# Taking all 512 columns in one matrix instruction in the projections and the first output product

## The chip, the cores and the metric

The program runs on one core of a Trainium2 chip. The time is device microseconds (us) of that core, the median of three runs. In the profile PE is the matrix engine (TensorE), PEld its weight loads, DVE is VectorE, ACT is ScalarE, POOL is GpSimd and SP issues the DMA transfers. PEclk is the clock that TensorE was granted, as a share of 2.4 GHz.

## The reference

Eight heads of attention in chunks of 64 positions give 4608 tokens of 512 features; two feed-forward layers follow. Cut to what matters:

```python
scores = q_c @ k_c.T / sqrt(64)              # per head and chunk of 64
attn = softmax(scores); x = attn @ v_c       # x: 4608 x 512
h = max(max(x @ w1, x @ w2), x @ w3)         # w1..w3: 512 x 768
y = h @ w_out                                # 768 x 512
g = max(y @ w_in, 0); g = g * g              # w_in: 512 x 2048
out = g @ w_out2                             # 2048 x 512
```

## The kernel before

The tokens are worked in nine blocks `b` of 512 (`TB`). Every product is made in three passes: each operand is split into a high part and a low part, both stored as fp32r, and high x high, high x low and low x high are added up in PSUM.

A *projection* is `proj` (L381): for one of six slices `f` of 128 features of h and one of the three matrices `w`, four blocks `k` of the inner dimension times three passes, into one PSUM tile `p` of 128 x 512. There are 9 x 6 x 3 = 162 of them, and two PSUM tiles `p`, used in turn. `p1_end` (L400) reads each tile out: `w` = 0 by a copy on ACT (L404), `w` = 1 by a maximum on DVE (L407), `w` = 2 by a maximum on DVE (L411), after which h is split into `hh` (ACT, L414) and `hl` (DVE, L416). The *first output product* is `g2` (L423): for each `(b, f)` four tiles `y` times three passes, added up over f in four PSUM tiles; after f = 5 they are copied out and sent to memory as `ys` (L433 to 438).

Both go through `mm_k` and `halves` (L365 to 379). `halves` takes each pass in pieces of `HC` = 256 columns, so a 512-column tile takes two instructions with the same stationary operand `lhs`, and each of them brings its own load of these weights. Two of the 162 projections, `(0, 0, 0)` and `(0, 0, 1)`, are called with `parts=2`: they are computed for each half of the block by itself, so there `dst` has 256 columns and `halves` makes one instruction per pass.

The later products, `z` (L461, y x w_in) and `g4` (L514, g x w_out2), write their own loops over 256 columns and do not go through `halves`. They use seven products for eight (a Strassen scheme), whose combined weights are prepared beforehand by `park` (L186; POOL adds at L161, ACT and DVE split at L210 and L212), stored, and fetched by `fetch` (L216) late in the projections.

The order: to about 165 us the order of all engines is written out by hand as a string of tokens. After that, `g2` and projections follow in loops over b and f, with one step of attention (scores S at L286, exponentials L293 to 299, sums L305 to 310, scaling on POOL at L313, transposition T at L319, output X at L347) beside each f, and the order within each engine is the framework's. The z products begin at about 675 us and the g4 products at about 1024 us. `heat` (L587) issues a few 128 x 512 bf16 products of zeros at the beginning.

Of the kernel before, what the change touches and what calls it, by code (L numbers as in the profile page):

```python
# [24 lines left out]
HC = 256  # L25
# [16 lines left out]
def kernel(ctx: ExitStack, tc, qkv, w123, w_out, w_in2, w_out2, out):  # L42


    nc = tc.nc
# [319 lines left out]
    def mm_k(dst, wpair, xpair, k, first, last):  # L365

        (wh, wl), (xh, xl) = wpair, xpair
        halves(dst, ((wh, xh), (wh, xl), (wl, xh)), first, last)

    def halves(dst, pairs, first, last):  # L370


        for j, (lhs, rhs) in enumerate(pairs):
            for i in range(dst.shape[-1] // HC):
                c = slice(i * HC, i * HC + HC)
                nc.tensor.matmul(  # L376
                    dst[:, c], lhsT=lhs, rhs=rhs[:, c], start=first and i == 0 and j == 0,
                    stop=last and j == len(pairs) - 1, skip_group_check=True,
                )

    def proj(wpair, xpair, name, parts=1):  # L381

# [215 lines left out]
    first = tc.manual_schedule()  # L598
# [138 lines left out]
    last = None  # L737
    more = iter(())
    for b in range(NB):
        for g in range(NG):  # L740
# [20 lines left out]
            last = (a, (b, g))  # L761
# [79 lines left out]
```

## Time and profile before

| what | value |
|---|---|
| runs | 1372.63 us median (1372.28 to 1373.52) |
| profiled execution: its own time | 1373.2 us |
| profiled execution: span | 1371.4 us, mean granted clock 0.997 |
| PE busy | 1356.9 us (99%), 13697 instructions |
| PEld busy | 1343.4 us (98%), 13699 instructions |
| DVE, ACT, POOL busy | 66%, 38%, 14% |
| DMA | 222.33 MB, mean 162 GB/s |

Busy time is the union of the records of an engine. Records of consecutive matrix instructions overlap, so the busy share of PE says that it had work, and the distance between two starts says how fast it went. In the views, `xN` at the end of a row is the number of instructions that it stands for.

### The profile page before, as it was taken

To read this page: it belongs to the slowest core of one execution; us is meant where nothing else is said; L and a number is where in the kernel's file an instruction comes from. 1 tells how busy PE (TensorE), PEld (TensorE's weight loads), DVE (VectorE), ACT (ScalarE), POOL (GpSimd) and SP (SyncE) were. 2 spreads that over 40 slices of the span, in tenths; PEclk is the share of its full clock that TensorE was granted. 3 is DMA by queue.
4 is the path that set the end of the run, shared out by engine and by line. 5 is a ranking of instruction groups with operands and counts; after the bars stand their busy time and mean duration, and the time that the engine had idled before them with its cause. 6 is when DMAs were issued, how large, how long until landed. Compare 5 with 4: busy or idle time off the path is not lost.

```text
span 1371.4 us, 32653 instructions
## 1 busy us (share of the span) xinstructions
PE 1356.9 (99%) x13697; PEld 1343.4 (98%) x13699; DVE 901.9 (66%) x1437; ACT 520.4 (38%) x904; POOL 194.5 (14%) x180
## 2 busy tenths in 40 slices
PE   7999999999999999999999999999999999999998
PEld 5999999999999999999999999999999999999998
DVE  7875565665665566622376666667667888878774
ACT  4643243343333333311233333333334444444442
POOL 3321133221432332300000000000000000000000
PEclk9999999999999999999999999999999999999999
DMA  9342353654644645617643334333598444444341
GB/s 280 123 137 81 124 182 125 227 159 154 213 142 166 219 140 180 220 55 239 198 148 124 129 141 147 139 139 141 189 345 315 149 146 132 131 139 149 130 139 46
DMA packets 101235, 222.33 MB, mean 162 GB/s; under 512 B 11232, under 2 KB 20448, under 8 KB 101088
## 3 DMA queue, kind: packets, MB, share of 16 engines
q1 hardware_dynamic: 101088, 220.25, 47.9%
q8 instruction: 107, 1.75, 0.5%
q14 instruction: 40, 0.33, 0.1%
HBM read 134.22 MB, written 85.98 MB: 161 GB/s over the span
## 4 chain that ended last, share of the span: by engine, by line
PE 86%; DVE 1%; issue 0%; POOLq 0%; POOL 0%; ACT 0%; DVEq 0%; ACTq 0%
PE z L471 25%; PE p L376 25%; PE o L522 25%; PE y L376 9%; PE X L347 1%; PE S L286 1%; PE T L319 1%; DVE pl L212 0%; DVE u L494 0%; POOL u L494 0%; POOLq L837 0%; DVE c L494 0%; DVE mx L293 0%; DVE sm L305 0%; DVE e L296 0%
## 5 line engine op out<-in xcount | busy, mean ns | idle before, releaser
L471 PE MATMUL z<-yxh,wih 128*128 128x256 f32 x560 | 155.4, 278 | 0.0
L471 PE MATMUL z<-yxh,wil 128*128 128x256 f32 x560 | 155.1, 277 | 0.0
L471 PE MATMUL z<-yxl,wih 128*128 128x256 f32 x560 | 155.1, 277 | 0.0
L522 PE MATMUL o<-wo2h,gl 128*128 128x256 f32 x504 | 139.2, 276 | 0.0
L522 PE MATMUL o<-wo2h,gh 128*128 128x256 f32 x504 | 139.2, 276 | 0.0
L522 PE MATMUL o<-wo2l,gh 128*128 128x256 f32 x504 | 139.2, 276 | 0.0
L522 PE MATMUL o<-wo2h,gxl 128*128 128x256 f32 x504 | 139.1, 276 | 0.0
L522 PE MATMUL o<-wo2l,gxh 128*128 128x256 f32 x504 | 139.1, 276 | 0.0
L522 PE MATMUL o<-wo2h,gxh 128*128 128x256 f32 x504 | 139.1, 276 | 0.0
L494 DVE TENSOR_TENSOR c<-z,s 128x512 f32<-128x512 f32 x108 | 74.4, 689 | 89.3 <-PE z L471 84.7
L414 ACT CAST hh<-h 128x512 fp32r<-128x512 f32 x54 | 33.4, 621 | 241.9 <-DVE h L411 223.8
L471 PE MATMUL z<-yh,wih 128*128 128x256 f32 x448 | 124.0, 277 | 0.0
L471 PE MATMUL z<-yh,wil 128*128 128x256 f32 x448 | 123.7, 276 | 0.0
L471 PE MATMUL z<-yl,wih 128*128 128x256 f32 x448 | 123.7, 276 | 0.0
L411 DVE TENSOR_TENSOR h<-p,m 128x512 f32<-128x512 f32 x54 | 37.1, 689 | 130.9 <-PE p L376 130.8
L494 POOL TENSOR_TENSOR u<-u,s 128x512 f32<-128x512 f32 x9 | 11.7, 1297 | 753.9 <-DVE u L494 753.9
L479 ACT COPY s<-z 128x512 f32<-128x512 f32 x108 | 63.5, 588 | 134.2 <-PE z L471 104.1
L471 PEld LDWEIGHTS z<-yxh,wih 128*128 128x128 f32 x560 | 105.3, 188 | 0.2 <-DVE c L494 0.2
L471 PEld LDWEIGHTS z<-yxl,wih 128*128 128x128 f32 x560 | 105.4, 188 | 0.0
L471 PEld LDWEIGHTS z<-yxh,wil 128*128 128x128 f32 x560 | 105.2, 188 | 0.0
L522 PEld LDWEIGHTS o<-wo2h,gxh 128*128 128x128 f32 x504 | 94.6, 188 | 0.0
L522 PEld LDWEIGHTS o<-wo2l,gh 128*128 128x128 f32 x504 | 94.6, 188 | 0.0
(184 smaller groups left out, 4056.5 us busy)
## 6 DMA issues: line engine op xcount, KB each, us to landing
gd<-g SPq DMA_DIRECT2D x144, 256.0 KB, 2.0
gr<-gd SPq DMA_DIRECT2D x72, 512.0 KB, 4.3
qk<-in_qkv SPq DMA_DIRECT2D x28, 512.0 KB, 4.1
raw<-in_w_out SPq DMA_DIRECT2D x22, 512.0 KB, 3.7
raw<-in_w SPq DMA_DIRECT2D x18, 512.0 KB, 4.0
v<-in_qkv SPq DMA_DIRECT2D x72, 128.0 KB, 5.6
yd<-ys SPq DMA_DIRECT2D x36, 256.0 KB, 2.9
yr<-yd SPq DMA_DIRECT2D x18, 512.0 KB, 5.1
```

The costliest lines, as they stand in the source:

```text
L286: nc.tensor.matmul(s_t[t][o:o + D, h ^ t % 2, :], lhsT=q[r, h, :], rhs=k[r, h, :], start=True, stop=True,)
L319: nc.tensor.transpose(tp[:, p * P:(p + 1) * P], e[:, 2 * p:2 * p + 2, :].rearrange("p h k -> p (h k)"), ident)
L347: nc.tensor.matmul(xps_t[t][j * D:j * D + D, p, c * D:c * D + D], lhsT=v[o:o + D, c, p, :], rhs=et[o:o + D, p, q:q + D], start=True, stop= ...
L376: nc.tensor.matmul(dst[:, c], lhsT=lhs, rhs=rhs[:, c], start=first and i == 0 and j == 0, stop=last and j == len(pairs) - 1, skip_group_ch ...
L411: nc.vector.tensor_tensor(out=h, in0=p, in1=st[b], op=ALU.max)
L414: nc.scalar.copy(hh, h)
L471: nc.tensor.matmul(dst[:, a * HC:a * HC + HC], lhsT=l[:, a, w], rhs=r[:, k, :], start=first and a + k + j == 0, stop=j == 2, skip_group_ch ...
L479: nc.scalar.copy(t, bank[tag])
L494: (eng or nc.vector).tensor_tensor(out=t, in0=x, in1=y, op=ALU.add)
L522: nc.tensor.matmul(bank[i][:, m * HC:m * HC + HC], lhsT=l[:, a, t], rhs=r[:, a, :], start=g + m + a + j == 0, stop=g == NG - 1 and j == 2, ...
```

## The change

In `halves` the loop over pieces of 256 columns is gone: each pass is one instruction over all columns of `dst`. Stationary operands, their order, the tiles and their places in memory stay as they were. `z`, `g4` and attention are untouched.

```diff
         for j, (lhs, rhs) in enumerate(pairs):
-            for i in range(dst.shape[-1] // HC):
-                c = slice(i * HC, i * HC + HC)
-                nc.tensor.matmul(
-                    dst[:, c], lhsT=lhs, rhs=rhs[:, c], start=first and i == 0 and j == 0,
-                    stop=last and j == len(pairs) - 1, skip_group_check=True,
-                )
+            nc.tensor.matmul(
+                dst, lhsT=lhs, rhs=rhs, start=first and j == 0, stop=last and j == len(pairs) - 1,
+                skip_group_check=True,
+            )
```

## Rows read from the trace of the kernel before

**Rows 1.** The page: the matrix engine's busy time, and the chain by line.

```profile
PE 1356.9 (99%) x13697; PEld 1343.4 (98%) x13699; DVE 901.9 (66%) x1437; ACT 520.4 (38%) x904; POOL 194.5 (14%) x180
...
PE z L471 25%; PE p L376 25%; PE o L522 25%; PE y L376 9%; PE X L347 1%; PE S L286 1%; PE T L319 1%; DVE pl L212 0%; DVE u L494 0%; POOL u L494 0%; POOLq L837 0%; DVE c L494 0%; DVE mx L293 0%; DVE sm L305 0%; DVE e L296 0%
```

**Rows 2.** Windows by stage: stretch, its length, busy us of each engine.

```profile
core 0: us, PE busy (x) PEld busy (x) DVE busy (x) ACT busy (x) POOL busy (x), PEclk, DMA share, GB/s
40.00:130.00 90.00, 89.80 (x855) 89.14 (x856) 61.90 (x102) 42.84 (x76) 26.19 (x20) 1.00 0.36 110
130.00:600.00 470.00, 469.67 (x5607) 463.79 (x5607) 284.00 (x458) 167.38 (x297) 132.01 (x126) 1.00 0.50 168
600.00:675.00 75.00, 75.00 (x664) 75.00 (x663) 19.40 (x29) 10.80 (x19) 0.00 (x0) 1.00 0.56 180
```

**Rows 3.** Groups by line, engine PE: busy us, mean ns of one.

```profile
L376 PE MATMUL p<-xh,w_0h 128*128 128x256 f32 x216 | 44.5, 281 | 0.0
...
L376 PE MATMUL y<-hh,wo0h 128*128 128x256 f32 x72 | 14.2, 278 | 0.0
```

**Rows 4.** The chain in order of time: start us, us, what.

```profile
445.52 2.94 PE p L376 x24
448.46 2.72 PE y L376 x24
451.18 5.44 PE p L376 x48
...
607.00 8.16 PE p L376 x72
615.16 2.72 PE y L376 x24
```

**Rows 5.** Timeline of PE and PEld: start us, us, engine, instruction, count.

```profile
400.30 0.30 PEld L376 LDWEIGHTS y<-hh,wo5l 128*128 128x128 f32 x2
400.41 0.39 PE L376 MATMUL y<-hh,wo5l 128*128 128x256 f32 x2
400.53 0.30 PEld L376 LDWEIGHTS y<-hh,wo5h 128*128 128x128 f32 x2
400.64 0.39 PE L376 MATMUL y<-hh,wo5h 128*128 128x256 f32 x2
```

**Rows 6.** Timeline of PEld at a first projection after a pause.

```profile
31.39 0.19 PEld L376 LDWEIGHTS p<-xh,w_0h 128*128 128x128 f32 x1
31.50 0.19 PEld L376 LDWEIGHTS p<-xl,w_0h 128*128 128x128 f32 x1
```

**Rows 7.** Timeline of PE at the same place.

```profile
31.40 0.38 PE L376 MATMUL p<-xh,w_0h 128*128 128x256 f32 x1
31.62 0.28 PE L376 MATMUL p<-xl,w_0h 128*128 128x256 f32 x1
31.73 0.29 PE L376 MATMUL p<-xh,w_0l 128*128 128x256 f32 x1
31.86 0.28 PE L376 MATMUL p<-xh,w_0h 128*128 128x256 f32 x1
```

**Rows 8.** One line's records in two stretches: ns least/median/most, first and last start.

```profile
L376 PE MATMUL p<-xl,w_5h x14: 281/281/281, 146.0 to 150.4; 128*128 128x256 f32 x14
...
L376 PE MATMUL p<-xh,w_1h x16: 276/276/276, 620.4 to 625.3; 128*128 128x256 f32 x16
```

**Rows 9.** Timeline of PE, 146.3 to 148.5 us.

```profile
146.47 0.40 PE L376 MATMUL p<-xh,w_5h 128*128 128x256 f32 x2
...
148.35 0.40 PE L376 MATMUL p<-xh,w_5l 128*128 128x256 f32 x2
```

**Rows 10.** Timeline of PE: products over 512 columns of bf16 zeros.

```profile
24.88 0.81 PE L590 MATMUL warm<-zero 128*128 128x512 bf16 x3 [0.16 <-issue]
25.52 0.60 PE L319 MATMUL T<-ident,e 128*128 128x128 f32 x4
```

**Rows 11.** Windows: 20 to 30 us, and 144.9 to 165.2 us.

```profile
20.00:30.00 10.00, 7.43 (x174) 6.50 (x175) 9.07 (x19) 5.10 (x11) 4.36 (x4) 1.00 1.05 257
...
144.90:165.20 20.30, 20.29 (x279) 19.64 (x277) 11.37 (x21) 6.05 (x11) 1.89 (x2) 1.00 0.41 131
```

**Rows 12.** Timeline, 561.5 to 563 us: a projection that waited.

```profile
561.67 0.68 DVE L407 TENSOR_TENSOR m<-p,s 128x512 f32<-128x512 f32 x1
...
562.40 0.30 PEld L376 LDWEIGHTS p<-xh,w_2h 128*128 128x128 f32 x2 [0.26 <-DVE m L407]
```

**Rows 13.** Waits of PE: us in total, times, longest.

```profile
PE T L319 <- POOL e L313: 1.4, 2, 1.2
```

## The prediction

> **What bounds the kernel now.** I read the page first: its shares and its chain [rows 1]. PE is busy for 99% of the span, and the chain that ended last runs over PE for nearly all its length, in four products: z, p, o and y. The change touches only p and y, a third of the chain together (25% and 9%). Next I read the windows by stage [rows 2], to see whether anything else is near its end where p and y run, from 31 us to about 675 us. It isn't: from 130 to 600 us DVE is busy for 284 of 470 us and ACT for 167, from 600 to 675 us the DMA share is 0.56, and PE is never short of work by more than 0.4 us in a stage. What PE saves there is therefore, to first order, taken off the end.
>
> The busy time does not tell how fast PE goes, since its records overlap. The chain in order of time does [rows 4]: where nothing comes between, 72 instructions p take 8.16 us and 24 instructions y take 2.72 us, so one instruction of 256 columns costs 113.3 ns, and one pass of 512 columns, two instructions, 226.7 ns. At the granted clock of 1.00, which is 2.4 GHz, 256 columns at one per cycle would take 106.7 ns. So 6.6 ns of each instruction are something other than columns. What that is decides this case.
>
> **What the 6.6 ns are.** Three views bear on it.
>
> The timeline of both rows of the engine [rows 5] shows one pattern everywhere: a weight load begins at the start of the product before its own (400.53 against 400.41 plus 0.113, that is 400.52), and its own product begins 0.11 us after it (400.64). Each load waits for the last to be taken over, and each product for its load: a ring of one load and one product.
>
> At the first projection after a pause [rows 6] the first load stands alone, with nothing streaming beside it, and the next load begins 0.11 us later, at 31.50. So a load alone already takes about as long as the whole step of 113 ns. The products beside them [rows 7] start at 31.62, 31.73 and 31.86: steps of 0.11 to 0.13 us, longer than the usual step for the same columns.
>
> The records of one line in two stretches [rows 8] are 276 ns at 620 us and 281 ns at 146 us, for one shape; in the stretch of 281 the step is 117.5 ns (1.88 us for 16 instructions [rows 9]). Columns cannot explain two speeds at one clock [rows 2, 11]; a product that sits a little longer before its weights are in can. After the pause the first record is even 0.38 us [rows 7], longer by just the 0.11 us of its load.
>
> So I read 256 columns as shorter than the load that is hidden beneath them, and the load as what sets the step. With 512 columns per load the order is the other way round: the load (0.11 us) ends long before the columns do.
>
> The Trainium skill, page "Perfetto Trace Analysis", section "Tensor Engine Instruction (MATMUL, LD_WEIGHTS)", speaks against leaning on the lengths of these records: the end of a matrix record is computed from the size of the instruction and not observed. The trace agrees only in part, since one size has 276, 281 and 380 ns here; if the rule held fully, the steps between starts would be left, and the rival of a fixed cost below would be as good as my reading.
>
> **The change part by part.** *Instructions removed.* There are 18 groups of p with 216 instructions and 18 of y with 72, one of each kind in [rows 3]: 3888 and 1296. Per projection that is 24, or 12 passes; the two projections in halves keep their 48 instructions. Joined are 160 x 12 = 1920 passes of p and 54 x 12 = 648 of y, together 2568. As many products and as many weight loads go.
>
> *Price of a joined pass.* The trace has no fp32r product over 512 columns. From below it is bounded by 512 columns at 2.4 GHz, 213.3 ns. The nearest row is the product of bf16 zeros over 512 columns [rows 10], each with its own load and at a granted clock of 1.00 [rows 11]: starts at 24.88 and, three products later, 25.52, so 213 ns each, 210 to 217 by the rounding. From above it is bounded by what two halves take, 226.7 ns, if the 6.6 ns belong to the columns; and by 226.7 plus some ns, if the load and the stream hinder each other (below). I take 217, the upper end of the nearest row, because a fixed cost can only add to the columns. Saved: 226.7 - 217 = 9.7 ns, times 2568 = 24.9 us. By the lower bound it would be 13.4 x 2568 = 34.4 us.
>
> The Trainium skill, page "TensorE: Matmul & The Clock Gate", section "Back-to-back issue gap", gives columns/2.4 + 2.5 ns for products back to back: 109.2 ns for 256 columns, 215.8 for 512. The trace has 113.3 for 256, so by that rule too something beside the products sets the step; an estimate with its 215.8 saves 10.9 x 2568 = 28.0 us.
>
> *The slow stretch.* Between 145 and 165 us PE goes at 117.5 ns, in some 147 instructions (279 of the window less 132 of attention [rows 11]), or 73 passes: 4.2 ns more for each instruction, 8.4 for each pass, 0.6 us that also goes.
>
> *Starts after attention.* The projection behind each attention step takes 2.94 us, not 2.72 [rows 4]: 0.11 is the bare first load, the rest the end of the product. Both stay: 0.
>
> *What becomes late.* A faster PE meets the others earlier. Two places had a wait already. At 562.40 us a projection waited for its PSUM tile, which DVE freed at 562.35 (0.26 us [rows 12]); DVE was behind with the splits of `park`, which do not come earlier. PE's work in a round of three projections and one output product, 10.9 us or 48 passes [rows 4], shrinks by 0.5 us, and the wait grows by that. Near 165 us the transpositions waited for POOL (1.4 us in two waits [rows 13], one of them early); with two thirds of those 73 passes before it, each shorter by 18 ns (235 to 217), 0.9 us could be lost, and I take half, because part of what DVE does there itself waits for PE. In the hand-written order from 40 to 130 us DVE is busy for 62 of 90 us [rows 2], which becomes 62 of 86; I allow 0.4 us. Together 1.4 us given back.
>
> *At no cost.* PSUM start and stop flags, the tiles' readers, DMAs and the number of waits stay: a reader waits for the last pass as before. The fetches of `fetch` have a DMA share of 0.56 to cover them [rows 2]; with 3% less time it is 0.58.
>
> **Sum.** 24.9 + 0.6 - 1.4 = 24.1 us. The profiled execution took 1373.2 us, its span being 1371.4 and 1.8 lying around it; 1373.2 - 24.1 = 1349.1. It stands 0.6 us (0.04%) above the median of the runs, so I give 1349.
>
> **Rivals.** 0.2%, about what a measurement can tell from no change, is 2.7 us here.
>
> *A, the load set the step (above).* 215 to 219 ns for a pass: 1344 to 1354. Chance 58%.
>
> *B, a fixed cost.* The 6.6 ns come with every instruction, whatever its columns. A joined pass costs 213.3 + 6.6 = 220 ns and saves 6.7 x 2568 = 17.2 us: 1373.2 - 17.2 + 0.8 = 1357. For it: the steady 113.3 in p and y, early and late. Against it: the second speed of 117.5. 17%.
>
> *C, no change.* The columns of fp32r themselves stream at 113.3 ns for 256. Then two halves and a whole cost the same, and the time stays at 1372 to 1374. For it: no row has fp32r at a faster step. Against: the records of 281 ns, and the load that alone takes 0.11 us. 9%.
>
> *D, slower: load and stream hinder each other.* After the pause, with a stream beside it, the step is up to 0.13 us where it settles at 0.113 [rows 7], so meeting badly costs some 17 ns. Now every load begins with its product and meets it at the same place, with the operands where they were. If the stream pays it, a pass costs 217 + 17 = 234 ns: 7.3 x 2568 = 18.8 us more, 1391. It decides from 9.7 ns upward; the 4.2 ns of the slow stretch would only bring it to about B (221). Against it: the settled state has only 6.6 ns for everything. 11%.
>
> *E, another order.* After 165 us the order on each engine is the framework's, and shorter instructions may move a step of attention or of `park`, with waits of some us: 1352 to 1366. The rows show one such wait in 500 us [rows 12]. 5%.
>
> **Range.** 1340 to 1364: from the lower bound of the pass (34.4 saved) past B and most of E; outside are C, D and ends of the others, a little over 2 in 10. Faster A + B + E, 80%; same C, 9%; slower D, 11%.
>
> **What would show it.** p as 1920 and y as 648 instructions of 128x512 (p with 48 of 128x256 left); 36 passes p in 7.8 us, where 8.16 stood; the weight loads 11131 in number, and PEld busy for about 87% (188 of 217 ns) from 600 us on, so that the load has slack; z and o in their old time. A step of 220 would mean B, of 227 C, of more D. The waits near 562 and 165 us should grow to about 0.8 us each. The prediction is wrong if the step of a joined pass is over 220, or if PE waits in p and y for over 3 us.

## The result, and the profile after

The change makes the kernel slower: 1387.64 us (median of four runs, 1387.48 to 1387.94) against 1373.08 us before (1372.28 to 1374.71), a ratio of 1.0102 with a 95% interval of 1.0090 to 1.0114, or 14.6 us. The forecast was 1349, a gain of 24 us. In one later set of runs (experiments 4 to 6) every kernel but that of experiment 6 took 11 to 13 us longer in some executions (the kernel before in 12 of 29, 1385.9 to 1388.7 us against 1372.6 to 1375.7), none of which was profiled, so that the cause is open; the times given there are medians of the other executions, 1374.3 us for the kernel before.

The page after, parts 1 and 4:

```profile
span 1386.0 us, 27572 instructions
PE 1371.1 (99%) x11129; PEld 1236.0 (89%) x11131; DVE 899.8 (65%) x1437; ACT 519.9 (38%) x904; POOL 192.8 (14%) x180
...
PE p L374 33%; PE z L469 25%; PE o L520 24%; PE y L374 11%; PE S L286 2%; PE X L347 2%; PE T L319 1%; DMA k<-in_qkv 1%; DVE xl L362 0%; PE warm L588 0%; POOL e L313 0%; DVE hl L414 0%; DVE u L492 0%; POOL u L492 0%; POOLq L835 0%
```

The change did what its diff says: 2568 matrix instructions fewer than in [rows 1], as many weight loads fewer, and the chain still runs over PE. The windows of the same stages (cut where they now lie) say whether PE waits for others:

```profile
40.00:130.00 90.00, 90.00 (x470) 72.65 (x471) 61.43 (x100) 42.69 (x76) 25.95 (x19) 1.00 0.38 109
130.00:614.00 484.00, 483.67 (x3770) 388.00 (x3770) 283.33 (x459) 167.05 (x297) 130.17 (x126) 1.00 0.50 163
614.00:689.00 75.00, 75.00 (x323) 60.45 (x322) 18.70 (x28) 10.58 (x18) 0.00 (x0) 1.00 0.55 178
```

It doesn't: PE lacks 0.33 us in the long stage, as before [rows 2], at the same clock, and DVE, ACT and the DMAs have no more to do. Only PEld has fallen, from all 75 us of the last stage to 60: by their records, the loads now have room. The time is in the products themselves, as the chain in order of time shows:

```profile
454.97 3.00 PE p L374 x12
457.97 2.80 PE y L374 x12
460.77 5.60 PE p L374 x24
...
620.21 8.40 PE p L374 x36
628.61 2.80 PE y L374 x12
```

36 joined passes p take 8.40 us where 72 halves took 8.16 [rows 4]: 233.3 ns for a pass, not 226.7, and not the 217 of the forecast. For y it is 2.80 for 2.72. The timeline of PE and PEld shows the rest of the picture:

```profile
400.38 0.40 PE L374 MATMUL p<-xh,w_5h 128*128 128x512 f32 x1
400.38 0.19 PEld L374 LDWEIGHTS p<-xl,w_5h 128*128 128x128 f32 x1
400.61 0.39 PE L374 MATMUL p<-xl,w_5h 128*128 128x512 f32 x1
400.62 0.19 PEld L374 LDWEIGHTS p<-xh,w_5l 128*128 128x128 f32 x1
```

The load begins with the product before its own, as in [rows 5], and by its record it is over after 0.19 us of 0.23. So the load seems to come in time, and the product is still no faster. This is a hint and no proof: a record of a load has 0.19 us also where the next load begins 0.11 us later [rows 6].

The sum of it: 2568 x 6.6 ns = 17.0 us more. Given back: the slow stretch before 165 us is gone (0.6), as forecast; the starts behind attention cost 3.00 - 2.80 = 0.20 us in place of 0.22 [rows 4], some 35 times (0.7, an estimate, since 0.02 us is close to what the rows resolve); and the wait near 562 us has gone (0.3). That leaves 15.4 of the measured 14.6. Most of the other 0.8 us lies behind p and y: by the timelines the first product z starts at 674.83 us before and at 690.05 after, 15.2 us later, and the last product o at 1366.41 and 1380.94, only 14.5 later. So the whole loss arises before z.

### The profile page after: what moved, and what is told of

It is laid out like the page before. It is cut to its first block, busy times and chain, and to the rows that moved or that the text cites. A ratio compares the mean times of both kernels' runs of the same rounds, so it can differ in the third digit from the quotient of the medians.

```text
span 1386.0 us, 27572 instructions
## 1 busy us (share of the span) xinstructions
PE 1371.1 (99%) x11129; PEld 1236.0 (89%) x11131; DVE 899.8 (65%) x1437; ACT 519.9 (38%) x904; POOL 192.8 (14%) x180
## 4 chain that ended last, share of the span: by engine, by line
PE 97%; DVE 1%; DMA 1%; issue 0%; ACT 0%; POOL 0%; SPq 0%; POOLq 0%; DVEq 0%
PE p L374 33%; PE z L469 25%; PE o L520 24%; PE y L374 11%; PE S L286 2%; PE X L347 2%; PE T L319 1%; DMA k<-in_qkv 1%; DVE xl L362 0%; PE warm L588 0%; POOL e L313 0%; DVE hl L414 0%; DVE u L492 0%; POOL u L492 0%; POOLq L835 0%
## 5 line engine op out<-in xcount | busy, mean ns | idle before, releaser
L520 PEld LDWEIGHTS o<-wo2h,gxl 128*128 128x128 f32 x504 | 94.6, 188 | 0.0
```

Source lines behind the costliest of these rows:

```text
L520: nc.tensor.matmul(bank[i][:, m * HC:m * HC + HC], lhsT=l[:, a, t], rhs=r[:, a, :], start=g + m + a + j == 0, stop=g == NG - 1 and j == 2, ...
```

## The experiments

### 1. The products by themselves

Is the step set by the load, by the columns, or by the two meeting? A stand-alone kernel in which nothing but PE works, with two tiles of real data:

```diff
+    def stretch(name, shift, n, count=24, cols=P):
+        t = ps.tile([P, 512], F32, tag="t", name=name, bufs=4)
+        for i in range(count):
+            w = i % 4 * P
+            nc.tensor.matmul(t[0:cols, 0:n], lhsT=wt[:, w:w + cols], rhs=mv[:, shift:shift + n], ...)
+    for j in range(16):
+        stretch("d" + ascii_letters[j], 8 * j, 512)
+        ...
```

> A stand-alone kernel: it leaves the whole computation out, loads one tile of real data, and lets the matrix engine alone run stretches of 24 fp32r products, each with its own weight load, with nothing on the other engines. In stretches da to dp it takes 512 columns, with the distance between the start of the moving operand and that of the weights going from 0 to 480 bytes (modulo 512) in steps of 32; in qa to qp the same with 256 columns; na to nd take 288, 320, 384 and 448 columns at 192 bytes, the distance in the kernel; ha and hb load 64 columns of weights in place of 128, at 192 and 0 bytes. Theory 1 (the load and the stream hinder each other, by the distance of their addresses): 512 columns take about 233 ns at 192 bytes, as in the changed kernel, and at some other distances about 216; with half the load (ha) the excess over 216 is about halved; 256 columns take 113.4 ns at 192 bytes and about 119 at 0, as the z products before show. Theory 2 (512 columns of fp32r always take this long): 233 ns at every distance, and with half the load too. Theory 3 (traffic of DVE, ACT or the DMAs slows the stream): about 216 ns at every distance, since all of them are idle here.

The timeline of PE; a step is the distance to the next start, divided by 24:

```profile
42.53 5.76 PE L64 MATMUL dg<-mv,wt 128*128 128x512 f32 x24
48.13 5.76 PE L64 MATMUL dh<-mv,wt 128*128 128x512 f32 x24
53.73 5.63 PE L64 MATMUL di<-mv,wt 128*128 128x512 f32 x24
59.19 5.77 PE L64 MATMUL dj<-mv,wt 128*128 128x512 f32 x24
...
115.40 2.89 PE L64 MATMUL qg<-mv,wt 128*128 128x256 f32 x24
118.13 3.00 PE L64 MATMUL qh<-mv,wt 128*128 128x256 f32 x24
120.97 3.04 PE L64 MATMUL qi<-mv,wt 128*128 128x256 f32 x24
123.84 3.00 PE L64 MATMUL qj<-mv,wt 128*128 128x256 f32 x24
...
159.41 5.71 PE L64 MATMUL ha<-mv,wt 128*64 128x512 f32 x24
164.95 5.68 PE L64 MATMUL hb<-mv,wt 128*64 128x512 f32 x24
```

At the kernel's distance of 192 bytes (dg) the step is (48.13 - 42.53)/24 = 233 ns, exactly the changed kernel's, with every other engine idle: theory 3 falls. At 256 bytes (di) it is 227.5, and the stretches from 256 bytes on repeat those from 0 on, so the distance counts modulo 256. That is against theory 2, but theory 1 fails as well: no distance comes near 216. With 256 columns, 192 bytes (qg) is the best of the map, 113.8, and 256 bytes (qi) has 119.6. Half the columns of weights (ha) change 233 to 231, far from half of the excess.

### 2. Which distance, and whose

> A stand-alone kernel again, with the computation left out: stretches of 16 fp32r products, each with its own weight load. Weights and moving operand are each put at 0, 32, .. 224 bytes modulo 256 (letters a to h, weights first, moving second: x_e_c has the weights at 128 and the moving operand at 64, as the projections of the kernel have them), x with 512 columns and q with 256. half and quart load 64 and 32 columns of weights; alone starts and stops with every product, so that nothing is added up in PSUM. Theory 1, after the first bench: every column of fp32r costs 113.3/256 ns (a floor of 226.7 for 512), and to that comes a hindrance of load and stream that goes by the distance of their addresses modulo 256. Then stretches with the same distance agree (x_e_c with x_f_d, x_a_g and so on, within 1 ns), none of 512 columns is under 226, and with 32 columns of weights all four places are within 2 ns of 226.7. Theory 2: the place of the moving operand by itself decides, whatever the load does. Then x_a_c to x_h_c agree, and fewer columns of weights change nothing. Theory 3: the floor too comes from the load (a load that is going on costs the stream 6.7 to 20 ns). Then with 32 columns of weights the step falls to about 217 to 220. If adding up in PSUM has a part in it, alone_e_c is below x_e_c.

Steps in ns from the starts in the timeline, 512 columns; rows are places of the weights, columns places of the moving operand, in bytes modulo 256:

```
            0    32    64    96   128   160   192   224
  0       241   234   229   233   233   234   233   232
 32       232   227   234   229   233   234   234   232
 64       233   233   228   234   229   233   233   234
 96       234   234   233   228   233   229   233   234
128       232   234   233   233   228   234   229   233
160       234   233   234   234   233   228   234   230
192       229   233   233   234   233   232   227   234
224       233   229   233   233   234   232   232   228
```

The diagonals agree (but for the first stretch, whose first step, behind the bf16 products of the start, takes 0.42 us; the granted clock had risen before it): the distance decides, not the place of either. Distance 0 has 227 to 228, 64 has 229 to 230, all others 232 to 234. The timeline for the kernel's own place and for the two views of adding up and of a quarter of the load:

```profile
135.54 3.90 PE L65 MATMUL x_e_c<-mv,wt 128*128 128x512 f32 x16
139.27 3.89 PE L65 MATMUL x_e_d<-mv,wt 128*128 128x512 f32 x16
143.00 3.81 PE L65 MATMUL x_e_e<-mv,wt 128*128 128x512 f32 x16
146.65 3.90 PE L65 MATMUL x_e_f<-mv,wt 128*128 128x512 f32 x16
...
389.91 3.86 PE L65 MATMUL quart_e_e<-mv,wt 128*32 128x512 f32 x16
393.60 3.87 PE L65 MATMUL quart_e_g<-mv,wt 128*32 128x512 f32 x16
397.31 3.89 PE L65 MATMUL alone_e_c<-mv,wt 128*128 128x512 f32 x16
401.03 3.81 PE L65 MATMUL alone_e_e<-mv,wt 128*128 128x512 f32 x16
```

With a quarter of the load the step is 231 ns at distance 0 (quart_e_e), more than with the whole load (x_e_e, 228), and 231 to 233 at the other three places. So theory 3 falls (the step does not sink to 217 to 220), and so does the part of theory 1 that wanted 226.7 there: the excess is no share of the load's time. The load has a part in it all the same: beside the whole load the step differs by 6 to 7 ns from place to place, beside the quarter by 2. Products that are not added up (alone_e_c, 232 to 233) are no faster.

### 3. Less load beside 256 columns, and more columns

> A stand-alone kernel, with the computation left out. full, half and quart: 256 columns of fp32r beside loads of 128, 64 and 32 columns of weights, at distances 128, 192, 0 and 64 (letters a, c, e, g). Theory 1 (the columns of fp32r set the step, 113.3 ns for 256, and the load fits beneath them): with a quarter of the load the step stays at 113.3 or above, at every distance. Theory 2, the one of the prediction (the load sets the step): with 64 and 32 columns of weights the step falls to 106.7 to 109 ns. na to ni: 256 to 512 columns in steps of 32 at distances 0 (e) and 192 (c). Theory 1: each 32 columns more cost 14.2 ns (17/16 of 13.3), although the load has ended by then, and the lines through them stand 0 to 7 ns above 113.3/256 for each column. Theory 2: 13.3 ns each, up to 217 for 512. bq, bn, bx: bf16 with 256, 384 and 512 columns: 216 for 512 as in the kernel's first products, 162 for 384, and for 256 about 109 if columns alone count. sa to sf: 256 columns at distances 192, 64, 0, 64, 192, 64, 32 products each: if the step is kept from what came before, 64 runs at 113.3 behind 192 and at 118 behind 0; if the distance alone decides, at 118 always.

The timeline, steps over 16 products:

```profile
12.21 2.08 PE L71 MATMUL full_e_e<-mv,wt 128*128 128x256 f32 x16
14.13 2.05 PE L71 MATMUL full_e_g<-mv,wt 128*128 128x256 f32 x16
16.02 2.02 PE L71 MATMUL half_e_a<-mv,wt 128*64 128x256 f32 x16
...
25.31 1.98 PE L71 MATMUL quart_e_c<-mv,wt 128*32 128x256 f32 x16
27.13 1.98 PE L71 MATMUL quart_e_e<-mv,wt 128*32 128x256 f32 x16
28.94 1.98 PE L71 MATMUL quart_e_g<-mv,wt 128*32 128x256 f32 x16
30.76 2.08 PE L71 MATMUL na_e<-mv,wt 128*128 128x256 f32 x16
...
36.61 2.29 PE L71 MATMUL nb_c<-mv,wt 128*128 128x288 f32 x16
38.74 2.50 PE L71 MATMUL nc_e<-mv,wt 128*128 128x320 f32 x16
...
77.19 3.90 PE L71 MATMUL ni_c<-mv,wt 128*128 128x512 f32 x16
80.93 1.92 PE L71 MATMUL bq_e<-mb,wb 128*128 128x256 bf16 x16
82.69 1.91 PE L71 MATMUL bq_c<-mb,wb 128*128 128x256 bf16 x16
...
89.64 3.62 PE L71 MATMUL bx_e<-mb,wb 128*128 128x512 bf16 x16
93.09 3.62 PE L71 MATMUL bx_c<-mb,wb 128*128 128x512 bf16 x16
```

This bears on the step of the prediction that failed. Beside a quarter of the weights, whose load has a record of 0.11 us for 0.19, 256 columns of fp32r still take 113 to 114 ns (quart_e_c, quart_e_e, quart_e_g), never the 107 to 109 of theory 2. So the length of the load does not set the step of the kernel's halves, which is 113.3 ns. The load has a part in what lies above that: beside the whole load the step is 120 ns at distance 0 (full_e_e) and 118 at 64 (full_e_g), beside the quarter 113 at both. Whether the last 6.7 ns need a load at all is not shown, since no product ran without one.

bf16 behaves as columns at 2.4 GHz should: (82.69 - 80.93)/16 = 110 ns for 256, 215.6 for 512. (Its load is shorter too, 0.10 us by its record, about that of the quarter load of fp32r.) fp32r does not: 288 columns take (38.74 - 36.61)/16 = 133 ns, 512 take 233.8. Of 32 columns more, I had expected 14.2 ns each time, and that was not quite it either. From the starts of single records the settled steps at 192 bytes are

```
columns             256    288    320    384    416    512
step, ns          113.4  133.3  146.8  173.3  186.7  233.3
columns/2.4 GHz   106.7  120.0  133.3  160.0  173.3  213.3
excess              6.7   13.3   13.5   13.3   13.4   20.0
```

At the granted clock of 1.00 these are the columns at 2.4 GHz, and to them come pieces of about 6.7 ns: one for 256 columns at this distance, two from 288 on, three for 512 (at distance 0: two for 256, two for 512). Other widths lie between (448 columns: 202, 15.5 ns of excess).

In the stretches sa to sf distance 64 ran at 118 every time, whatever came before; but 192 ran at 117.8 behind bf16 and at 113.3 in another place. So for one distance there can be two rhythms, and my question was put to the wrong one. The products that run at 117.8 ns (sa_c) have records of 281 ns, those at 113.3 (se_c) of 276, as in [rows 8].

### 4. The distance in the whole kernel

The joined kernel and the kernel before, each with x moved by 64 bytes, from distance 192 to 0 (cut: `xl` and the sizes of two other tiles change too, so that what lies behind x keeps its place modulo 256):

```diff
+    def wide_tile(tag, name, shift):
+        t = ap.tile([P, KD * TB + 64], F32R, tag=tag, name=name)
+        return t[:, shift:shift + KD * TB].rearrange("p (k n) -> p k n", k=KD)
...
-                    ap.tile([P, KD, TB], F32R, tag="xh", name=f"xh{b}"),
+                    wide_tile("xh", f"xh{b}", 16),
```

> The changed kernel with the projections' moving operands (x, high and low) moved by 64 bytes, so that their distance to the weights is 0 modulo 256 and not 192; the tiles behind them stay where they were modulo 256. Theory 1 (a floor of 113.3 ns for every 256 columns of fp32r, and a hindrance by the distance): the 1920 joined passes of p go from 233.4 to 226.7 ns, which is 12.8 us, so 1375; the 648 of y keep 233.4. Theory 2 (in the full kernel 512 columns take 233 ns anyway, because of the other engines or the order): 1387 to 1388.

> The kernel before with the same move of the projections' moving operands by 64 bytes. Theory 1: at distance 0 an instruction of 256 columns takes 120.0 ns in the bench, 6.6 more than at 192; with 3888 of them in p that is 25.7 us, so 1399: the move that helps the joined passes harms the halves. Theory 2: 1373.

Measured: 1378.1 and 1398.4 us, against 1374.3 for the kernel before. The chain in the joined kernel, then in the halved one:

```profile
601.10 8.18 PE p L378 x36
609.28 2.80 PE y L378 x12
```

```profile
630.26 8.62 PE p L380 x72
638.88 2.74 PE y L380 x24
```

The same move takes the joined p from 8.40 to 8.18 us (227 ns for a pass) and the halved p from 8.16 to 8.62 (239 ns for a pass), and leaves y, whose operands did not move, at 2.80 and 2.74. Theory 2 falls for both. For the halved kernel the sum is right (1398.4 for 1399; it is 24.1 over the kernel before of this set, for 25.7). The joined one is 3 us over 1375: p averages 227.6 ns from start to start over all its passes, not 226.7, which is 1.7 us, and the kernel before lies 1.2 us higher in this set than in the first. So with a distance that suits it the joined p costs what the halves cost at theirs, and what is left of the loss is mostly y.

### 5. Only y joined

The kernel before, in which only the call for y asks for pieces of `TB` columns (cut to that line):

```diff
-            mm_k(yacc[b][d], (wh[:, a, c], wl[:, a, c]), hp, f, f == 0, f == NF1 - 1)
+            mm_k(yacc[b][d], (wh[:, a, c], wl[:, a, c]), hp, f, f == 0, f == NF1 - 1, TB)
```

> The kernel before with only the first output product joined (648 passes at distance 192), the projections in halves. Theory 1: each joined pass costs 233.4 for 226.7, 648 x 6.7 = 4.3 us more, 1377.4. A theory in which the loss comes from the projections' neighbours (attention, PSUM readers) would leave it at 1373.

Measured: 1377.5 us, 3.2 over the kernel before, where 4.3 were expected. The chain:

```profile
609.47 8.16 PE p L376 x72
617.63 2.79 PE y L376 x12
```

Each product pays for itself: y 2.79 for 2.72 us, p unchanged. The time alone proves little, since the runs of before spread over 3 us and the profiled execution of this kernel took only 1375.5; the row is the evidence.

### 6. EARLY at 0

The products z and o have, in 252 places (240 in z, 12 in o), an operand shifted by 192 bytes (EARLY), which puts them at distance 0.

```diff
-EARLY = 48
+EARLY = 0
```

> The kernel before, with the first of the seven operands of z and o no longer moved by 192 bytes in the wide tiles, so that these 252 products are at the same distance as all others of their line. Theory 1: they go from about 119 to 113.4 ns: 1.4 us less, 1371.7. Theory 2: no change, 1373.

A miss: 1385.61 us, some 11 us slower than the kernel before, where 1.4 us less were expected. The chain, here and in the kernel before:

```profile
680.56 351.80 PE z L471 x2987
...
1035.25 337.41 PE o L522 x2977
```

```profile
680.99 339.45 PE z L471 x2975
...
1024.77 337.86 PE o L522 x2977
```

From start to start the 240 products z went from about 120 ns to 117.7, not to 113.4, and the other 2784, whose distance of 192 is unchanged, from 113.6 to 117.7. So halves have two rhythms there, and without the products at distance 0 z ran in the slow one: 11 us over the 3024 products z. o, which lost its 12, stayed in the fast one (337.41 us for 2977 products, 337.86 before). So products at distance 0 are not needed for the fast rhythm everywhere, and how they keep z in it, if it is they that do, is not shown.

### 7. Is there a distance at which joining wins?

> A stand-alone kernel, with the computation left out: the map of distances in steps of 4 bytes (0 to 252; the distance is 32 times the first letter plus 4 times the second, counted from 0), 16 fp32r products of 512 columns each (x), then of 256 (q). The steps so far are the columns at 2.4 GHz plus multiples of about 6.7 ns: 113.3 is 106.7 and one, 120 two; 226.7 is 213.3 and two, 233.3 three. Theory 1 (two such pieces are the least for 512 columns): no distance is under 226, and joining can't gain anywhere. Theory 2 (the count depends on the distance alone, and steps of 32 bytes missed the good ones): some distance has 220 or 213 ns for 512 columns, and a joined kernel with its operands there would be faster than the kernel before.

Of 64 distances, none was under 226.7 ns for 512 columns (settled steps, from the starts of single records); 226.7 came at seven of them, up to 240 at others. 256 columns had 113.3 at three (16, 144 and 192 bytes). Theory 1 holds: the best joined pass costs what two halves cost at the kernel's distance. No version in these experiments beats the kernel before.

## Why the prediction was wrong

*What bounds the kernel* held: PE, and all of its loss or gain in p and y reaches the end.

*The step that failed* is "I read 256 columns as shorter than the load that is hidden beneath them, and the load as what sets the step". From it followed that a joined pass, with columns longer than its load, would be nearly free of the excess. Beside a quarter of the load the halves still take 113 ns, and products whose columns outlast the load have more excess and not less: 13.3 ns for 288 columns (experiment 3), 20 for the joined pass, where the forecast had 4. In [rows 5, 6] load and product are equally long, and I took the one for the cause of the other; a first load that takes 0.11 us alone shows that the load fits in the step, not that it makes it. The 276 and 281 ns of [rows 8] go with two rhythms, 113.3 and 117.8 ns, which one shape has at one distance with the same load (experiment 3), so they do not show a product that waits for a longer load.

*The price of a joined pass* (217 ns, measured 233.3) was then read off a row of bf16 [rows 10]. bf16 has 215.6 in the bench too; fp32r has 226.7 to 240. A neighbour in shape, but not in type, was the wrong row. That the operands stay where they are, at a distance of 192 bytes, was in the forecast only as a rival; it is 6.6 of the 233.3 ns (experiment 4).

*The rivals.* B (17%) took the excess as fixed; it is 6.7 ns for 256 columns, 13.3 for 288 and 20 for 512 (experiment 3). E (5%) did not come: PE lacks 0.33 us from 130 to 614 us, as in the long stage before. C (9%) had the right floor: two halves or a whole, 226.7 at best. D (11%) had the right sign and, as it turned out, the right price, 234 ns, and its condition, operands that meet badly because they stay where they were, was confirmed by the move of x (experiment 4). But its price was right by luck: its sum was another one, 217 and 17 there, 226.7 and 6.6 here, and the 17 ns came from the first products after a pause. Nor does the stream pay for the length of the load: a quarter of it makes the pass cheaper by 1 to 2 ns at 192 bytes and dearer by 3 at 0 (experiment 2). The chances were the wrong way round: steps of 0.12 to 0.13 us after a pause [rows 7] and the slow stretch [rows 8, 9] both showed that the same columns can take longer, and I used both for A.

*What becomes late*: of 1.4 us forecast, about 0.2, because PE became slower. The wait near 562 us vanished; POOL's waits went from 1.4 [rows 13] to 1.6 us:

```profile
PE T L319 <- POOL e L313: 1.6, 2, 1.3
```

*The slow stretch* (0.6 us) went as forecast. z and o stayed within 1 us: z takes 349 us, all PE, as before.

The Trainium skill, page "TensorE: Matmul & The Clock Gate", section "Back-to-back issue gap", whose 215.8 ns I had set beside my 217, agrees with the bf16 stretches (215.6 for 512, 110 for 256) and with no fp32r stretch (226.7 or more). The same section of the Trainium skill gives this formula for an isolated product, and about 131 ns for 512 columns in a stream of loads and products; no stretch of 512 columns here is under 215.6. The same page of the Trainium skill says (Part 2, "Step-by-step: what each phase is for") that loading the next weights takes no SBUF read bandwidth from the running product; the runs show a step that goes by the distance between the two operands' addresses, 228 at 0 and 233 at 192 bytes, so the two do not run side by side unhindered, though no run shows whether it is the reading that is hindered. As to the lengths of records, the Trainium skill, page "Perfetto Trace Analysis", section "Tensor Engine Instruction (MATMUL, LD_WEIGHTS)", has a delay of SBUF in the computed end beside the size, which the prediction left out; so 276 and 281 ns for one size do not speak against it.

*Open* are what the pieces of 6.7 ns are, whether they would be there without a load beside the product, why 512 columns have three of them at 192 bytes where two halves have one each, and what chooses between the two rhythms of the halves.

## What to carry to other kernels

Two rows that are equally long do not tell which sets the pace; shorten one of them by itself and see whether the step moves, before a sum is built on it. Take the price of a new shape from a row of the same type, or measure it in a stand-alone stretch: here one such run gave the changed kernel's 233 ns. Fewer and larger instructions gain nothing where small ones already run at the floor, and the addresses that suit the one shape need not suit the other.

## What the runs showed of the hardware

- The step of an fp32r product depends on the distance of its moving operand from the weights modulo 256 bytes, and not on either place: 226.7 to 240 ns for 512 columns, 113.3 to 123 for 256, each beside a load of 128 columns of weights. Beside a load of 32 the places differ little: 231 to 233 for 512 columns, 113 to 116 for 256. The same move of 64 bytes helps the one (233 to 227) and harms the other (113 to 120). bf16 has 215.6 at both distances that were tried.
- One shape at one distance can run in two rhythms, 113.3 and 117.7 ns, for hundreds of us. The run in which z lost its 240 products at another distance had all of z in the slower one, 11 us more; what chooses between the two is not shown.
